# The end of the weight conversion on GpSimd, and the late units' activations turned by TensorE

## The chip, the cores and the metric

The kernel runs on one core of a Trainium2 chip. The metric is the device time of one execution in microseconds (us), median of the runs. Engines are named as the profile names them: PE is TensorE (PEld its weight loads), DVE is VectorE, ACT is ScalarE, POOL is GpSimd, SP is SyncE, which issues most of the DMAs here.

## What is computed

An mLSTM cell over 4 batches, 8 heads, 768 positions, head size 40; its output, 3072 tokens of 320 channels, goes through a multiplicative feed-forward network. From the reference, shortened:

```
for t in range(S):                       # mLSTM cell, per batch and head
    m_new  = maximum(f[t] + m, i[t])
    f_stab = exp(f[t] + m - m_new);  i_stab = exp(i[t] - m_new);  m = m_new
    C = f_stab * C + i_stab * outer(v[t], k[t])
    n = f_stab * n + i_stab * k[t]
    y[t] = sigmoid(o_gate[t]) * (C @ q[t]) / maximum(abs(n . q[t]), 1)

x = y as (3072 tokens, 320 channels)
h = ((x @ w1) * (x @ w2)) @ w3           # w1, w2: 320 x 1024, w3: 1024 x 1024
out = h @ w_out                          # 1024 x 320
```

The four weights arrive in float64; everything else is float32.

## The kernel before

**Units and steps.** The cell is computed in chunks. A unit is 128 positions of one batch (all 8 heads): 24 units, unit n being batch n mod 4. One loop of 30 steps, counted from 0, pipelines everything. Step s does the scores and the state update of unit s and the outputs of unit s-1 (both in `quarter_work`, into one PSUM tile named cell), turns the output y of an earlier unit into xT (channels on partitions), runs some of the up products (`up`, `up_rest`: x @ w1 into pa and x @ w2 into pb, multiplied into ab), and from step 17 on some of the down products (`ffn_out`: ab @ w3o into po, then the output DMA). `n_up` and `n_down` say how many of each: one up in steps 3 to 6, two from step 7 on; two downs in steps 17 to 26.

**Order.** TensorE's instructions are chained in program order (`in_order`). For the other engines a scheduler orders them by priorities, `tc.issue_after` moving some behind others; for everything up to and including step 6 (`pinned = 7`), `keep_order` fixes them in program order as well. In one step VectorE does: L348 (scores times weights), L352 and L357 (state), L368 and L372 (h), L377 to L380 (den), L382 and L384 (y), then conversions, and L568 (ab). GpSimd does: L280 (two selects on pw of the next unit), L302 (vw), L307 (decay of the state, twice a unit: once ahead of the step's products, once between L352 and L357), L412 (the doubling of y's last 64 channels).

**From y to xT.** For units 0 to 14 (n < NY = 15) `twice` copies y's last 64 channels behind themselves on GpSimd (L412), so that the last, half-filled block of channels lies on both halves of the partitions, and `x_trans` turns three blocks of 128 on TensorE into px and copies px to xT on ScalarE (L422). For units 15 to 23 `send` and `get_back` write y to DRAM and read it back in another order, and `x_turn` transposes it on VectorE (L408).

**Conversion of weights.** A weight piece of 128 x 512 (or 128 x 320 for w_out) comes as pairs of 32-bit words into raw (four buffers; `fetch`). `scale` (L175, ScalarE) scales the high words in place. `to_f32` then makes float32 out of both words in five passes on VectorE: L186 and L187 put sign and shifted exponent and mantissa into t (tile ex), L188 keeps the sign and exponent of t in r (tile ma), L189 multiplies the low words into r, L190 adds t and r into the result. `n_cvt` says how many conversions follow in each step: two in step 4 and 5, three in steps 6 to 8, two after that, to step 15. Pieces of w1 and w2 come first, then w_out, then two for each of eight blocks of w3; the latter are transposed on VectorE (L239, w3T), and `fold` makes w3o = w3 @ w_out of them on TensorE (`w3_mm`, into wp), a block a step, in steps 10 to 17.

**PSUM.** pa, pb, px, pt, wp and po share four banks in turn; cell has four of its own. After step 24 these are added to the turn.

**Names in the profile.** Tiles are named as in the code: gates is one tile of [128, 2 * TB] that holds the gate vectors at the start and, from unit 17 on, the k and q that are loaded for `turn`; between them it is not used.

Of the kernel before, what the change touches and what calls it, by code (L numbers as in the profile page):

```python
# [8 lines left out]
FP = mybir.dt.float32  # L9
U32 = mybir.dt.uint32  # L10
AF = mybir.ActivationFunctionType
OP = mybir.AluOpType
# [4 lines left out]
def kernel(  # L17
# [91 lines left out]
    wT = const.tile([P, NT2, BH], FP, name="wT")  # L109
    decay = const.tile([P, B * NP, NT], FP, name="decay")  # L110
    U_d = dram.tile([NT, BH, L], FP, name="U_d")
    NY = 15
    KC = KF + 1
    y_d = [dram.tile([P, 4, KC, 32], FP, name=f"y_d{n}") if n >= NY else None for n in range(NU)]

    o_t, u_t = {}, {}

# [56 lines left out]
        hi = raw[:, :, 1].bitcast(FP)  # L174
        nc.scalar.mul(out=hi, in_=hi, mul=2.0 ** -111)  # L175

    def to_f32(dst, raw):

        n = dst.shape[-1]
        lo, hi = raw[:, :, 0], raw[:, :, 1]
        t = wst.tile([128, n], U32, name="ex", tag="ex", bufs=1)
        r = wst.tile([128, n], U32, name="ma", tag="ma", bufs=1)
        V = nc.vector
        V.tensor_scalar(out=t, in0=hi, scalar1=3, scalar2=None, op0=OP.logical_shift_left)  # L186
        V.scalar_tensor_tensor(out=t, in0=hi, scalar=0x80000000, in1=t, op0=OP.bitwise_and, op1=OP.bitwise_or)  # L187
        V.tensor_scalar(out=r, in0=t, scalar1=0xFF800000, scalar2=None, op0=OP.bitwise_and)  # L188
        V.scalar_tensor_tensor(out=r.bitcast(FP), in0=lo, scalar=2.0 ** -52, in1=r.bitcast(FP), op0=OP.mult, op1=OP.mult)  # L189
        V.tensor_tensor(out=dst, in0=t.bitcast(FP), in1=r.bitcast(FP), op=OP.add)  # L190

    def cols(c0, n):
# [32 lines left out]
        scaled.append(pend.pop(0))  # L225
        scale(scaled[-1][1])

    def convert():
        if not scaled:
            scale_next()  # L230
        dst, raw, ko, half = scaled.pop(0)
        if dst is not None:
            to_f32(dst, raw)
            return
        w3 = wst.tile([128, CW], FP, name="w3", tag="w3")
        to_f32(w3, raw)
        if half == 0:
            w3T_t[ko] = wst.tile([128, FO, 128], FP, name="w3T", tag="w3T")
        nc.vector.transpose(out=w3T_t[ko].rearrange("c k (m r) -> c m k r", r=32)[:, 2 * half:2 * half + 2],  # L239
                            in_=w3.rearrange("r (m k c) -> r m k c", m=2, k=FO))  # L240
        if half:
            turned_w3.append(ko)

    def fold():
# [54 lines left out]
    def weighted(n):  # L299
        c, b = divmod(n, B)  # L300
        vw_t[n] = sb.tile([P, H, D1], FP, name="vw", tag="vw")
        nc.gpsimd.tensor_tensor(out=vw_t[n], in0=vbuf[n % NB], op=OP.mult,  # L302
                                in1=wT[:, c, b * H:(b + 1) * H].unsqueeze(2).to_broadcast([P, H, D1]))

    def decayed(new, old, n, x):
        c, b = divmod(n, B)
        nc.gpsimd.tensor_tensor(out=new, in0=old, op=OP.mult, in1=decay[:, b * NP:(b + 1) * NP, 2 * c + x:2 * c + x + 1]  # L307
                                .to_broadcast([P, NP, D1]))
# [55 lines left out]
    def outputs(n, pi, ph):  # L364
# [6 lines left out]
        for x, r in enumerate(halves):  # L371
# [11 lines left out]
        y_t[n] = sb.tile([P, DM + REM], FP, name="y", tag="y")  # L383
        return nc.vector.tensor_tensor(out=y_t[n][:, 0:DM].rearrange("p (h d) -> p h d", d=D), in0=h[:, :, 0:D], in1=e,  # L384
                                op=OP.mult)

    def send(n):


        y = y_t.pop(n)  # L390
        for cc in range(KF):
            nc.sync.dma_start(out=y_d[n][:, :, cc, :], in_=y[:, cc * P:(cc + 1) * P].rearrange("t (i c) -> t i c", c=32))
        for i in range(0, 4, 2):
            nc.sync.dma_start(out=y_d[n][:, i:i + 2, KF, :], in_=y[:, KF * P:DM].rearrange("t (i c) -> t i c", c=32))

    back_t = {}

    def get_back(n):
        back_t[n] = sb.tile([P, 4, KC, 32], FP, name="yb", tag="yb", bufs=1)
        for i in range(4):  # L400
            nc.sync.dma_start(out=back_t[n][32 * i:32 * (i + 1)].rearrange("r m k c -> r m (k c)"),
                              in_=y_d[n][:, i].rearrange("(m r) k c -> r m (k c)", r=32))

    def x_turn(n):
        gr, j = divmod(n, GT)
        if j == 0:
            x_t[gr] = ffn.tile([128, KC, TG], FP, name="xT", tag="xT")
        nc.vector.transpose(out=x_t[gr][:, :, j * P:(j + 1) * P].rearrange("c k (m r) -> c k m r", r=32),  # L408
                            in_=back_t.pop(n).rearrange("r m k c -> r k m c"))

    def twice(n):
        nc.gpsimd.tensor_copy(out=y_t[n][:, DM:DM + REM], in_=y_t[n][:, KF * P:DM])  # L412
# [173 lines left out]
    w12 = [("w12", i, part) for part in range(2) for i in range(2 * KF + 1)]  # L586
    todo = w12[KF * 2 + 1:] + [("wo", i, 0) for i in range(FO)] + [("w3", ko, part) for ko in range(FO) for part in range(2)]
    n_cvt = [2, 1, 1, 1, 2, 2, 3, 3, 3] + [2] * 7
    pinned = 7
    behind = ExitStack()  # L590
    turned, converted, fetched = 0, 2, 2 * KF + 1

    for s in range(len(n_up)):
        if B <= s + 3 < NU:
            load_u(s + 3)
        if s + 2 < NU:
            load(s + 2)
            load_o(s + 2)
        if 0 < s < B - 1:
            weights(s + 1)  # L600
            out_gate(s)
        if s < NU:
            weighted(s)
            if s >= B:
                decayed(state[s % B][1], state[s % B][0], s, 0)
            if 0 < s < N_DVE:
                turn(s)
        if NY <= s - 2 < NU:
            send(s - 2)
        elif 0 <= s - 2 < NY:  # L610
            twice(s - 2)
        if N_DVE <= s + 1 < NU:
            load_turned(s + 1)
        if NY <= s - 2 < NU:
            get_back(s - 2)
        while turned < min(s - 2, NY):
            x_trans(turned)
            turned += 1
        fold()
        for _ in range(n_down[s]):  # L620
            ffn_out(*downs.pop(0))
        now = [ups.pop(0) for _ in range(n_up[s])]
        open_ups = [up(*x) for x in now]
        if len(now) == 1 and turned == s - 2 < NY:
            x_trans(turned)
            turned += 1

        def rest():
            for x in open_ups:
                up_rest(*x)  # L630

        gated = None
        if s <= NU:
            gated = quarter_work(s, rest)
        else:
            rest()
        with tc.issue_after(gated.ins) if gated else nullcontext():
            if NY <= s - 2 < NU:
                x_turn(s - 2)
            if N_DVE <= s + 1 < NU:  # L640
                turn(s + 1)
        if s == 0:
            gate_cols(g, gT, nc.scalar.copy)
            out_gate(0)
            scale_next()
            weights(1)
        if s == NU:
            cell_psum.close()
            banks.append(ctx.enter_context(tc.tile_pool(name="ps_x", bufs=4, space=bass.MemoryType.PSUM)))
        if B - 1 <= s < NU:  # L650
            if s + 1 < NU:
                weights(s + 1)
            out_gate(s)
        for _ in range(n_cvt[s] if s < len(n_cvt) else 0):
            convert()
            converted += 1
        while todo and fetched < converted + (2 if s < 2 else 3):
            fetch(*todo.pop(0))
            fetched += 1
        if s + 1 == pinned:  # L660
            for ins in keep_order(front):
                behind.enter_context(tc.issue_after(ins))
# [30 lines left out]
```

## Time and profile before

| | |
|---|---|
| median of 3 runs | 485.59 us (484.08 to 487.2) |
| the profiled execution: time | 485.59 us |
| the profiled execution: span of the trace | 483.8 us |
| mean granted clock of TensorE | 0.975 |
| busy: PE, PEld, DVE, ACT, POOL | 94%, 77%, 55%, 29%, 18% of the span |
| DMA | 49.31 MB, mean 102 GB/s |

The span is what the trace covers, from the first to the last instruction; the time of the execution is 1.8 us longer. The page gives busy shares of the whole span and of 40 slices, the chain of work that ended last, and groups of instructions by line and tile. A timeline line reads: start, length, engine, line, operation, output<-inputs, shapes, how many, and in brackets how long the engine had been idle before it and what ended that. A line of the waits reads: engine, line, what it waited for, us in total, times, longest. Busy time by stretch gives, for each engine, busy us and instructions in brackets, then the granted TensorE clock, the busy share of the DMA engines, and GB/s.

### The profile page before, as it was taken

The numbers are of one execution on the slowest core, as the hardware profiler recorded it, in microseconds if no ns is written. First come the engines' busy times: TensorE is split into PE (matmuls) and PEld (weight loads), VectorE is DVE, ScalarE is ACT, GpSimd is POOL, SyncE is SP. The second block draws the span as 40 slices with busy tenths as digits, with TensorE's granted clock in tenths as the row PEclk, the third lists the DMA queues.
The fourth block names the chain that finished last, engine by engine and source line by source line (L and its number), as shares of the span: only waits on it lengthen the run. The fifth ranks groups of instructions, "written<-read, shape, count | busy, mean of one in ns | idle before, by whom it ended". The sixth has DMA issues, their size and how long they took to land.

```text
span 483.8 us, 13400 instructions
## 1 busy us (share of the span) xinstructions
PE 453.1 (94%) x5631; PEld 370.5 (77%) x5631; DVE 265.3 (55%) x535; ACT 142.0 (29%) x390; POOL 85.8 (18%) x156
## 2 busy tenths in 40 slices
PE   3859897989899999999999999999999999999997
PEld 2758786989687887888877787877877778778864
DVE  7886698899859788877660515336154242211110
ACT  3733553633433442524531212021100011011011
POOL 5431222712303211322320202110000000000000
PEclk9797998989899999999999999999999999999999
DMA  8999937678955947630455255462331211200001
GB/s 182 175 182 214 164 88 141 119 151 192 189 107 128 182 100 154 134 82 15 87 109 115 58 122 127 96 134 54 89 93 24 62 31 31 61 14 15 1 15 41
DMA packets 135772, 49.31 MB, mean 102 GB/s; under 512 B 116320, under 2 KB 126752, under 8 KB 135712
## 3 DMA queue, kind: packets, MB, share of 16 engines
q1 hardware_dynamic: 132112, 44.42, 46.8%
q10 hardware_dynamic: 3600, 4.03, 2.4%
q8 instruction: 44, 0.72, 0.7%
q14 instruction: 16, 0.13, 0.1%
HBM read 42.63 MB, written 5.80 MB: 100 GB/s over the span
## 4 chain that ended last, share of the span: by engine, by line
PE 75%; DVE 11%; issue 6%; DMA 3%; POOL 2%; SPq 1%; ACT 1%; DVEq 0%; POOLq 0%; ACTq 0%
PE po L90 22%; PE pa L90 21%; PE pb L90 14%; PE wp L90 8%; PE cell L90 7%; PE pt L93 2%; DVE h L372 2%; DMA pw<-U_d 1%; DMA kbuf<-in_k_dram 1%; PE ub L90 1%; SPq L170 1%; DVE ma L189 1%; DVE ex L187 1%; DVE o_in L382 1%; POOL pw L280 1%
## 5 line engine op out<-in xcount | busy, mean ns | idle before, releaser
L568 DVE TENSOR_TENSOR ab<-pb,a_sb 128x512 f32<-128x512 f32 x48 | 32.9, 690 | 149.6 <-ACT a_sb L567 149.4
L90 PE MATMUL po<-w3o,ab 128*128 128x320 f32 x384 | 106.2, 435 | 0.0
L90 PEld LDWEIGHTS po<-w3o,ab 128*128 128x128 f32 x384 | 72.1, 190 | 30.1 <-issue 0.4
L90 PE MATMUL pa<-xT,w 128*128 128x256 f32 (+1 forms) x448 | 94.2, 358 | 0.7 <-ACT xT L422 0.7
L90 PE MATMUL pb<-xT,w 128*128 128x256 f32 (+1 forms) x448 | 92.5, 353 | 0.7 <-issue 0.7
L90 PEld LDWEIGHTS pa<-xT,w 128*128 128x128 f32 x448 | 78.2, 199 | 11.8 <-ACT xT L422 1.1
L90 PEld LDWEIGHTS pb<-xT,w 128*128 128x128 f32 x448 | 76.8, 194 | 8.4
L567 ACT ACTIVATE a_sb<-pa 128x512 f32<-128x512 f32 x48 | 28.6, 597 | 148.2 <-PE pb L90 148.2
L90 PE MATMUL pa<-xT,wr 64*64 64x256 f32 (+1 forms) x448 | 48.2, 357 | 0.0
L90 PE MATMUL pb<-xT,wr 64*64 64x256 f32 (+1 forms) x448 | 48.2, 357 | 0.0
L307 POOL TENSOR_TENSOR state<-state,decay 128x164 f32<-128x164 f32 x40 | 19.5, 492 | 150.1 <-issue 53.7
L278 ACT ACTIVATE pw<-pw,aT 128x64 f32<-128x64 f32 x160 | 40.6, 337 | 18.2 <-DMA pw<-U_d 18.2
L280 POOL TENSOR_SCALAR_AFFINE_SELECT pw<-pw 64x512 f32<-64x512 f32 x48 | 36.5, 760 | 46.8 <-ACT pw L278 45.2
L90 PEld LDWEIGHTS pa<-xT,wr 64*64 64x64 f32 x448 | 29.2, 136 | 15.0 <-issue 7.0
L90 PE MATMUL wp<-wo,w3T 128*128 128x320 f32 x128 | 37.5, 448 | 2.0 <-DVE w3T L239 2.0
L90 PEld LDWEIGHTS wp<-wo,w3T 128*128 128x128 f32 x128 | 24.6, 197 | 11.8 <-issue 3.5
L575 ACT COPY o_sb<-po 128x320 f32<-128x320 f32 x24 | 10.2, 424 | 76.9 <-PE po L90 76.9
L90 PEld LDWEIGHTS cell<-vbuf,pw 64*64 64x64 f32 x768 | 26.9, 139 | 4.2 <-issue 2.0
L90 PEld LDWEIGHTS pb<-xT,wr 64*64 64x64 f32 x448 | 29.2, 136 | 0.0
L90 PE MATMUL cell<-vbuf,pw 64*64 64x41 f32 x768 | 26.8, 228 | 1.4 <-issue 1.4
L348 DVE TENSOR_TENSOR pw<-cell,pw 128x512 f32<-128x512 f32 x24 | 16.4, 684 | 15.7 <-PE cell L90 13.2
L372 DVE TENSOR_TENSOR h<-cell,h 64x328 f32<-64x328 f32 x48 | 23.8, 497 | 1.0
(90 smaller groups left out, 481.3 us busy)
## 6 DMA issues: line engine op xcount, KB each, us to landing
raw<-in_moe_w_dram SPq DMA_DIRECT2D x64, 128.0 KB, 3.2
pw<-U_d SPq DMA_DIRECT2D x40, 128.0 KB, 3.9
kbuf<-in_k_dram SPq DMA_DIRECT2D x24, 160.0 KB, 4.0
vbuf<-in_v_dram SPq DMA_DIRECT2D x24, 160.0 KB, 4.8
o_in<-in_o_gate_dram SPq DMA_DIRECT2D x24, 160.0 KB, 3.4
out_dram<-o_sb ACTq DMA_DIRECT2D x24, 160.0 KB, 2.0
raw<-in_moe_w_dram SPq DMA_DIRECT2D x7, 512.0 KB, 5.9
qbuf<-in_q_dram SPq DMA_DIRECT2D x17, 160.0 KB, 4.9
```

Source lines behind the costliest of these rows:

```text
L90: in_order(nc.tensor.matmul(out, lhsT=lhsT, rhs=rhs, start=start, stop=stop))
L93: in_order(nc.tensor.transpose(out, in_, ident[0:n, 0:n]))
L170: nc.sync.dma_start(out=dst, in_=src)
L187: V.scalar_tensor_tensor(out=t, in0=hi, scalar=0x80000000, in1=t, op0=OP.bitwise_and, op1=OP.bitwise_or)
L278: nc.scalar.activation(out=pw[:, h, :], in_=src[:, h, :], func=AF.Exp, bias=aT[:, c, b * H + h:b * H + h + 1])
L280: nc.gpsimd.affine_select(out=pw[r], in_=pw[r], compare_op=OP.is_ge, fill=0.0, base=0, pattern=[[0, H], [1, L]], channel_multiplier=-1)
L307: nc.gpsimd.tensor_tensor(out=new, in0=old, op=OP.mult, in1=decay[:, b * NP:(b + 1) * NP, 2 * c + x:2 * c + x + 1] .to_broadcast([P, NP, D1]))
L348: first_read = nc.vector.tensor_tensor(out=pv, in0=ss, in1=pv, op=OP.mult)
L372: nc.vector.tensor_tensor(out=h[r], in0=ph[x], in1=h[r], op=OP.add)
L567: nc.scalar.mul(out=a_sb, in_=pa, mul=UP ** -2)
L568: nc.vector.tensor_tensor(out=ab_t[gr][j][:, fs[0]:fs[-1] + 1, t0:t0 + a_sb.shape[-1]], in0=pb, in1=a_sb, op=OP.mult)
L575: nc.scalar.copy(out=o_sb, in_=po)
```

## The change

Two things are changed.

In steps 4 to 14 the last two conversions of each step take another form (`to_f32` with E). t and r are no longer tiles of their own but the first two slices of 512 columns of gates, the same two for every such conversion. The three first passes stay on VectorE. ScalarE then scales the low words in place, and the last two passes, a product and a sum, run on GpSimd. A piece of w3 converted so is transposed a step later (`unturned`, `turn_w3`), and with it `fold` comes to that block a step later. GpSimd's share of unit n for n > 4 (`weigh`: L302 and the first L307) is written at the end of step n-1, ahead of the conversions, instead of at the start of step n.

Units 15 to 23 no longer go through DRAM: `send`, `get_back` and `x_turn` are gone, and `twice` and `x_trans` serve all 24 units.

```
@@ -109,9 +109,7 @@
     wT = const.tile([P, NT2, BH], FP, name="wT")
     decay = const.tile([P, B * NP, NT], FP, name="decay")
     U_d = dram.tile([NT, BH, L], FP, name="U_d")
-    NY = 15
     KC = KF + 1
-    y_d = [dram.tile([P, 4, KC, 32], FP, name=f"y_d{n}") if n >= NY else None for n in range(NU)]
 
     o_t, u_t = {}, {}
 
@@ -174,19 +172,27 @@
         hi = raw[:, :, 1].bitcast(FP)
         nc.scalar.mul(out=hi, in_=hi, mul=2.0 ** -111)
 
-    def to_f32(dst, raw):
+    def to_f32(dst, raw, E=None):
 
 
 
         n = dst.shape[-1]
         lo, hi = raw[:, :, 0], raw[:, :, 1]
-        t = wst.tile([128, n], U32, name="ex", tag="ex", bufs=1)
-        r = wst.tile([128, n], U32, name="ma", tag="ma", bufs=1)
+        if E is None:
+            t = wst.tile([128, n], U32, name="ex", tag="ex", bufs=1)
+            r = wst.tile([128, n], U32, name="ma", tag="ma", bufs=1)
+        else:
+            t, r = (gates[:, i * CW:i * CW + n].bitcast(U32) for i in range(2))
         V = nc.vector
         V.tensor_scalar(out=t, in0=hi, scalar1=3, scalar2=None, op0=OP.logical_shift_left)
         V.scalar_tensor_tensor(out=t, in0=hi, scalar=0x80000000, in1=t, op0=OP.bitwise_and, op1=OP.bitwise_or)
         V.tensor_scalar(out=r, in0=t, scalar1=0xFF800000, scalar2=None, op0=OP.bitwise_and)
-        V.scalar_tensor_tensor(out=r.bitcast(FP), in0=lo, scalar=2.0 ** -52, in1=r.bitcast(FP), op0=OP.mult, op1=OP.mult)
+        if E is None:
+            V.scalar_tensor_tensor(out=r.bitcast(FP), in0=lo, scalar=2.0 ** -52, in1=r.bitcast(FP), op0=OP.mult, op1=OP.mult)
+        else:
+            V = E
+            nc.scalar.mul(out=lo.bitcast(FP), in_=lo, mul=2.0 ** -52)
+            V.tensor_tensor(out=r.bitcast(FP), in0=lo.bitcast(FP), in1=r.bitcast(FP), op=OP.mult)
         V.tensor_tensor(out=dst, in0=t.bitcast(FP), in1=r.bitcast(FP), op=OP.add)
 
     def cols(c0, n):
@@ -225,20 +231,30 @@
         scaled.append(pend.pop(0))
         scale(scaled[-1][1])
 
-    def convert():
+    def convert(E=None):
+
         if not scaled:
             scale_next()
         dst, raw, ko, half = scaled.pop(0)
         if dst is not None:
-            to_f32(dst, raw)
+            to_f32(dst, raw, E)
             return
         w3 = wst.tile([128, CW], FP, name="w3", tag="w3")
-        to_f32(w3, raw)
-        if half == 0:
+        to_f32(w3, raw, E)
+        if ko not in w3T_t:
             w3T_t[ko] = wst.tile([128, FO, 128], FP, name="w3T", tag="w3T")
+        if E is None:
+            turn_w3(w3, ko, half)
+        else:
+            unturned.append((w3, ko, half))
+
+    unturned, halves_in = [], {}
+
+    def turn_w3(w3, ko, half):
         nc.vector.transpose(out=w3T_t[ko].rearrange("c k (m r) -> c m k r", r=32)[:, 2 * half:2 * half + 2],
                             in_=w3.rearrange("r (m k c) -> r m k c", m=2, k=FO))
-        if half:
+        halves_in[ko] = halves_in.get(ko, 0) + 1
+        if halves_in[ko] == 2:
             turned_w3.append(ko)
 
     def fold():
@@ -384,30 +400,6 @@
         return nc.vector.tensor_tensor(out=y_t[n][:, 0:DM].rearrange("p (h d) -> p h d", d=D), in0=h[:, :, 0:D], in1=e,
                                 op=OP.mult)
 
-    def send(n):
-
-
-        y = y_t.pop(n)
-        for cc in range(KF):
-            nc.sync.dma_start(out=y_d[n][:, :, cc, :], in_=y[:, cc * P:(cc + 1) * P].rearrange("t (i c) -> t i c", c=32))
-        for i in range(0, 4, 2):
-            nc.sync.dma_start(out=y_d[n][:, i:i + 2, KF, :], in_=y[:, KF * P:DM].rearrange("t (i c) -> t i c", c=32))
-
-    back_t = {}
-
-    def get_back(n):
-        back_t[n] = sb.tile([P, 4, KC, 32], FP, name="yb", tag="yb", bufs=1)
-        for i in range(4):
-            nc.sync.dma_start(out=back_t[n][32 * i:32 * (i + 1)].rearrange("r m k c -> r m (k c)"),
-                              in_=y_d[n][:, i].rearrange("(m r) k c -> r m (k c)", r=32))
-
-    def x_turn(n):
-        gr, j = divmod(n, GT)
-        if j == 0:
-            x_t[gr] = ffn.tile([128, KC, TG], FP, name="xT", tag="xT")
-        nc.vector.transpose(out=x_t[gr][:, :, j * P:(j + 1) * P].rearrange("c k (m r) -> c k m r", r=32),
-                            in_=back_t.pop(n).rearrange("r m k c -> r k m c"))
-
     def twice(n):
         nc.gpsimd.tensor_copy(out=y_t[n][:, DM:DM + REM], in_=y_t[n][:, KF * P:DM])
 
@@ -586,9 +578,14 @@
     w12 = [("w12", i, part) for part in range(2) for i in range(2 * KF + 1)]
     todo = w12[KF * 2 + 1:] + [("wo", i, 0) for i in range(FO)] + [("w3", ko, part) for ko in range(FO) for part in range(2)]
     n_cvt = [2, 1, 1, 1, 2, 2, 3, 3, 3] + [2] * 7
-    pinned = 7
+    pinned, early = 7, 4
     behind = ExitStack()
     turned, converted, fetched = 0, 2, 2 * KF + 1
+
+    def weigh(n):
+        weighted(n)
+        if n >= B:
+            decayed(state[n % B][1], state[n % B][0], n, 0)
 
     for s in range(len(n_up)):
         if B <= s + 3 < NU:
@@ -600,20 +597,15 @@
             weights(s + 1)
             out_gate(s)
         if s < NU:
-            weighted(s)
-            if s >= B:
-                decayed(state[s % B][1], state[s % B][0], s, 0)
+            if s <= early:
+                weigh(s)
             if 0 < s < N_DVE:
                 turn(s)
-        if NY <= s - 2 < NU:
-            send(s - 2)
-        elif 0 <= s - 2 < NY:
+        if 0 <= s - 2 < NU:
             twice(s - 2)
         if N_DVE <= s + 1 < NU:
             load_turned(s + 1)
-        if NY <= s - 2 < NU:
-            get_back(s - 2)
-        while turned < min(s - 2, NY):
+        while turned < min(s - 2, NU):
             x_trans(turned)
             turned += 1
         fold()
@@ -621,7 +613,7 @@
             ffn_out(*downs.pop(0))
         now = [ups.pop(0) for _ in range(n_up[s])]
         open_ups = [up(*x) for x in now]
-        if len(now) == 1 and turned == s - 2 < NY:
+        if len(now) == 1 and turned == s - 2 < NU:
             x_trans(turned)
             turned += 1
 
@@ -635,8 +627,6 @@
         else:
             rest()
         with tc.issue_after(gated.ins) if gated else nullcontext():
-            if NY <= s - 2 < NU:
-                x_turn(s - 2)
             if N_DVE <= s + 1 < NU:
                 turn(s + 1)
         if s == 0:
@@ -651,8 +641,12 @@
             if s + 1 < NU:
                 weights(s + 1)
             out_gate(s)
-        for _ in range(n_cvt[s] if s < len(n_cvt) else 0):
-            convert()
+        if early <= s < NU - 1:
+            weigh(s + 1)
+        while unturned:
+            turn_w3(*unturned.pop(0))
+        for i in range(n_cvt[s] if s < len(n_cvt) else 0):
+            convert(nc.gpsimd if i + 2 >= n_cvt[s] and early <= s < len(n_cvt) - 1 else None)
             converted += 1
         while todo and fetched < converted + (2 if s < 2 else 3):
             fetch(*todo.pop(0))
```

## The prediction

> **What bounds the kernel now.** Steps are counted from 0; step s does the quarter work of unit s. I read the engine totals first, then busy time by step (cut at the starts of L348, the first thing VectorE does with a step's scores), then the waits of TensorE, then the timelines of the steps where it waits.
>
> ```profile
> PE 453.1 (94%) x5631; PEld 370.5 (77%) x5631; DVE 265.3 (55%) x535; ACT 142.0 (29%) x390; POOL 85.8 (18%) x156
> ```
>
> 94% is a mean over stages. By step, from L348 of step 3 to L348 of step 11, and later, over nine full steps:
>
> ```profile
> 48.71:60.19 11.48, 9.11 (x205) 8.32 (x205) 8.10 (x18) 6.48 (x18) 3.19 (x6) 1.00 1.07 162
> 60.19:72.32 12.13, 11.12 (x227) 10.60 (x226) 10.94 (x22) 6.34 (x17) 3.25 (x6) 1.00 0.39 90
> 72.32:83.64 11.32, 8.02 (x184) 7.27 (x184) 10.12 (x23) 3.55 (x12) 3.25 (x6) 0.85 0.76 140
> 83.64:101.26 17.62, 15.39 (x281) 14.97 (x280) 16.06 (x35) 10.29 (x31) 8.93 (x14) 0.93 0.62 122
> 101.26:112.87 11.61, 11.61 (x255) 11.42 (x255) 10.75 (x27) 4.11 (x13) 3.65 (x6) 0.96 0.98 188
> 112.87:126.97 14.10, 13.57 (x214) 11.63 (x211) 13.10 (x28) 6.83 (x18) 2.64 (x5) 1.00 0.92 195
> 126.97:147.03 20.06, 18.25 (x215) 14.41 (x216) 13.11 (x28) 5.71 (x16) 2.86 (x5) 0.91 0.69 125
> 147.03:163.80 16.77, 16.77 (x221) 13.81 (x220) 14.17 (x30) 6.62 (x19) 3.99 (x7) 1.00 0.76 150
> ...
> 271.40:411.00 139.60, 139.60 (x1446) 109.75 (x1445) 53.59 (x108) 21.92 (x56) 10.14 (x17) 1.00 0.36 80
> ```
>
> Columns: length, busy PE, PEld, DVE, ACT, POOL, clock, DMA. VectorE sets the pace from step 4 to about 128 us; from step 10 on TensorE has no gap, so there only its own instructions count. Where TensorE waits:
>
> ```profile
> PE px L93 <- DVE y L384: 4.5, 3, 3.3
> ...
> PE pt L93 <- DVE ab L568: 2.2, 1, 2.2
> PE wp L90 <- DVE w3T L239: 2.0, 1, 2.0
> ```
>
> Step 5 of the timeline, GpSimd and then TensorE, carries the forecast:
>
> ```profile
> 61.20 0.47 POOL L307 TENSOR_TENSOR state<-state,decay 128x164 f32<-128x164 f32 x1 [6.69 <-DVE state L352]
> 61.61 1.38 POOL L280 TENSOR_SCALAR_AFFINE_SELECT pw<-pw 64x512 f32<-64x512 f32 x2
> 63.07 0.74 POOL L302 TENSOR_TENSOR vw<-vbuf,wT 128x328 f32<-128x328 f32 x1
> 63.77 0.46 POOL L307 TENSOR_TENSOR state<-state,decay 128x164 f32<-128x164 f32 x1
> 65.61 0.36 POOL L412 COPY y<-y 128x64 f32<-128x64 f32 x1 [1.38 <-DVE y L384]
> ...
> 65.69 0.67 PE L93 MATMUL px<-ident,y 128*128 128x128 f32 x3 [1.01 <-DVE y L384]
> ```
>
> y of unit 3 ends on VectorE at 65.55 (65.06 + 0.49), GpSimd doubles its tail at once (L412), and the third px transpose reads that tail. TensorE is in order: behind px stand the rest of the up products, then cell, then L348. So step 5 hangs on a loop: L348, y, L412, px, cell, next L348.
>
> What idling costs TensorE, one step later:
>
> ```profile
> 75.00:77.80 2.80, 0.00 (x0) 1.00 1.38 186
> 77.80:79.50 1.70, 1.68 (x23) 0.63 0.48 116
> 79.50:81.50 2.00, 2.00 (x44) 0.50 0.20 49
> 81.50:83.60 2.10, 2.10 (x112) 0.97 0.52 159
> ```
>
> [...] L302 at 328 elements takes 0.74, L307 at 164 takes 0.46, so 512 by the line through them is 1.05. [...] on 96x256 tiles L506 takes 0.42, L508 and L510 0.72 and 0.83 while GpSimd runs L507 and L509. [...] Above, 3.3 us of idling is followed by 0.50. [...] Seen above: L307 waits 6.69 us to 61.20, and the selects behind it start only then, though their ScalarE input was complete at 58.48 (56.47 + 2.01).
>
> **The change part by part.** In steps 4 to 14 two conversions each (22 in all) lose L189 and L190 on VectorE and get one ScalarE scaling and two GpSimd passes. That frees VectorE 0.69 + 0.69 a conversion of 512 columns, about 30 us in all. But the two new tiles are fixed slices of gates, one set for all. The order of instructions on each engine shows what follows:
>
> (a) VectorE's first pass of the second conversion (B) overwrites what GpSimd's last pass of the first (A) reads, so it waits. In series now: A's three passes on VectorE, two on GpSimd, B's three, two on GpSimd.
>
> (b) On GpSimd the four passes of step s stand ahead of the L412 copy that belongs to step s+1. In steps 5 and 6, where px needs that copy in the same step, px waits for all of (a). In step 7 the px of that unit comes only in step 8; nothing waits.
>
> Step 4 to 5, from L348 at 60.19. y ends 65.55, A's passes (0.42, 0.69, 0.43, starting 65.46) end 67.07. GpSimd: start after 0.08, as L307 after L352 here; two passes at 1.1[...] to 69.35. B to 71.04, GpSimd to 73.32, copy to 73.66. From third px to L348: 3.72 here at full clock (65.98 to 69.7), but TensorE has then idled 7 us, so I take the 5.35 of the next step (78.10 to 83.45), which followed such an idle. L348 at 79.0 instead of 72.32: +6.7. Step 5 to 6, counted from its L348: A (512) done 6.88, GpSimd 9.16, B (320 columns: 0.33, 0.49, 0.33) 10.45, GpSimd 2 x 0.74 to 12.05, copy 12.38, plus 5.35 gives 17.7 against 11.32: +6.4. Together +13.1.
>
> Steps 6 to 10. VectorE's sum from L348 of step 6: chain to y 5.4; the conversion still whole 2.25; A 1.2; wait 1.7; B 1.2; three passes 1.2; ab 0.7. That makes 13.6, where ab releases the qT transposes (L93) at 98.62 - 83.64 = 15.0 today: TensorE 1.4 ahead, less idle. In step 7 GpSimd is late (selects, vw and decays stand behind the conversions), which costs VectorE about 2.6 us of waiting at B; in step 9 the transposes wait for ab until 42.5 on this count. Then comes a gain: the first w3T is now turned a step later, so step 10 has no wp, and neither the 2.0 us wait nor its slow start (6.24 where the later ones take 4.31) arises. The up products of step 10 start at 43.3 on this count, against 51.0 today, of which 4.3 is the wp that moves to step 17. -3.4 at best, -1.8 if the clock dips; I take -3.0.
>
> Steps 11 to 17 stay at 16.8: VectorE with its two waits of 2.3 comes to about 15, and w3T is ready a step ahead. ScalarE's 22 scalings at the 0.635 of L175 (14 us) lie in an engine busy 40% of these steps.
>
> Units 15 to 23: nine times three transposes return to TensorE, where nothing hides them. At 163.92 px starts and wp at 164.24: 0.33 each, +3.0. Taken away are nine VectorE transposes of 0.57 and 72 DMA issues on SP, and added are nine copies on GpSimd and nine on ScalarE: all beside a TensorE that never waits here, worth nothing either way.
>
> Moving vw and the first decay a step earlier costs nothing by itself: GpSimd did them at that place already (63.07). Its raw tiles come free later by some 2 us; they are fetched a step ahead, so 0, or +2 if ScalarE's queue stands behind a late one.
>
> Sum: 13.1 - 3.0 + 3.0 = +13.1. The profiled execution took 485.59 with a span of 483.8, and 485.59 is also the median: 498.7.
>
> Bounds. A GpSimd pass could be 1.05 (-0.4 on eight passes) or 1.3 (+1.5[...]). A warm clock would take 3.2 off. Steps 6 to 10 lie between -8 and +3.
>
> **The rivals.** (1) The forecast, 498.7. (2) The relief decides: VectorE stops being the bound from step 6 to 10 and TensorE runs back to back: steps of 12.4, 12.7 and 12.4 plus 1.2 to step 10's first up product are 38.7 where today's count is 46.7: -8.0. Speaking for it are the VectorE shares of those steps; against it, the serial waits of (a). With the queue at +13.1 it gives 493.7; with a clock that also stays warm, 490.5, about 1% slower. (3) Faster or level: GpSimd is so quick that the queue costs nothing. The two steps then are 25.2 + 7.3p (p is one pass of 512; the sum above with p left open) against 23.45, warm. With rival 2's -8.0 and the +3.0 it turns at p = 0.45; at 0.3 it gives 484.5. Two-input passes in this trace are far above that. (4) The change as meant, copy not behind the conversions: steps 5 and 6 would gain 1.0, total 484.6. The order on GpSimd speaks against it. (5) The late copies and waits spread: VectorE past 16.8 in steps 11 to 16 by 1 us each: 504.7.
>
> **How the numbers follow.** Forecast 0.62, rival 2 0.17, rivals 3 and 4 0.03 each, rival 5 0.15. About 1% is what a measurement of this kernel can tell from no change. Slower by over 1%: rivals 1 and 5 and most of 2, 0.89; within 1%: 0.08; faster: 0.03. The range runs from rival 2 with a clock partly warm (491) to near rival 5 (504).
>
> **What would show it.** Right: in steps 5 and 6 px waits for GpSimd's y copy, some 7 us each, half clock after it, those steps 17 to 19 us long; VectorE waits for GpSimd at the first pass of every second conversion; no wp in step 10, two in step 17; from step 11 on TensorE full, about 0.33 longer a step from step 18. Wrong: if these two steps stay under 14 us, or if steps 6 to 9 shrink by more than 5, or if TensorE has gaps after step 11.

## The result, and the profile after

The changed kernel takes 512.1 us, the median of 4 runs (509.07 to 513.54), against 485.78 for the kernel before: a ratio of 1.0535, 95% interval 1.047 to 1.06. The forecast was 498.7 with a range up to 504, so the sign was right and the size was half of what happened. The profiled execution of the changed kernel took 509.07 with a span of 507.4. It is the quickest of the four; the sums below are made against spans, 507.4 - 483.8 = 23.6.

Line numbers moved with the edit: y is now L400 (was L384), the first work on a step's scores L364 (L348), the y copy L404 (L412), ab L560 (L568), the decay of the state L323 (L307). The engine totals of after first:

```profile
PE 460.1 (91%) x5658; PEld 375.7 (74%) x5658; DVE 237.2 (47%) x482; ACT 158.4 (31%) x421; POOL 135.4 (27%) x209
```

VectorE has 28.1 us less work (265.3 before), and TensorE's busy share fell from 94% to 91%. Busy time by stretch of after, cut at the starts of L364 of steps 4, 5 and 6, at that of step 17, and at the end (columns as before: length, PE, PEld, DVE, ACT, POOL, clock, DMA share, GB/s):

```profile
60.19:79.88 19.69, 10.31 (x204) 9.62 (x204) 8.24 (x18) 5.27 (x16) 8.16 (x10) 0.74 0.64 115
79.88:99.75 19.87, 11.64 (x204) 10.90 (x204) 7.85 (x18) 7.52 (x21) 7.35 (x10) 0.71 0.45 81
99.75:290.81 191.06, 184.44 (x2511) 153.57 (x2512) 118.04 (x240) 81.96 (x217) 86.32 (x113) 0.99 0.54 111
290.81:507.40 216.59, 212.01 (x1851) 164.12 (x1850) 58.05 (x115) 34.42 (x81) 11.84 (x25) 1.00 0.18 45
```

The same two long stretches of before:

```profile
83.64:271.50 187.86, 183.29 (x2511) 153.68 (x2510) 136.99 (x277) 73.10 (x202) 47.52 (x76) 0.98 0.59 121
271.50:483.80 212.30, 209.02 (x1824) 161.52 (x1824) 62.24 (x124) 30.11 (x72) 10.04 (x17) 1.00 0.26 61
```

These cuts are worth copying: TensorE has the same 2511 instructions between step 6 and step 17 in both kernels (the block of wp products that moved to step 17 stays inside), so the lengths can be subtracted. In both kernels step 4 starts its scores' work at 60.19. So the 23.6 us are: steps 4 and 5, 39.56 against 23.45 (12.13 + 11.32), +16.1; steps 6 to 16, 191.06 against 187.86, +3.2; the rest, 216.59 against 212.30, +4.3. The forecast had +13.1, -3.0 and +3.0.

What TensorE and VectorE wait for in after:

```profile
DVE w3T L254 <- POOL w L196: 18.4, 7, 2.9
...
PE px L93 <- POOL y L404: 15.6, 2, 8.4
...
PE pt L93 <- DVE ab L560: 4.2, 5, 1.9
...
DVE gates L187 <- POOL w L196: 2.8, 1, 2.8
...
PE po L90 <- DVE h L388: 1.3, 1, 1.3
```

The second line is the queue that the forecast named: px of steps 5 and 6 waits 15.6 us in two pieces for a copy of 0.24 us. GpSimd in step 5, then the px that it releases:

```profile
67.20 1.29 POOL L195 TENSOR_TENSOR gates<-raw,gates 128x512 f32<-128x512 f32 x1 [2.97 <-issue]
68.56 1.26 POOL L196 TENSOR_TENSOR w<-gates 128x512 f32<-128x512 f32 x1
71.61 1.29 POOL L195 TENSOR_TENSOR gates<-raw,gates 128x512 f32<-128x512 f32 x1 [1.78 <-issue]
72.97 1.26 POOL L196 TENSOR_TENSOR w<-gates 128x512 f32<-128x512 f32 x1
74.18 0.24 POOL L404 COPY y<-y 128x64 f32<-128x64 f32 x1
...
74.47 0.47 PE L93 MATMUL px<-ident,y 128*128 128x128 f32 x1 [8.38 <-POOL y L404]
```

y itself is ready on VectorE at 65.54 (65.05 + 0.49). Between the second and the third line VectorE does the three first passes of the next conversion, and starts them only when GpSimd has left the shared tile:

```profile
69.86 0.43 DVE L187 TENSOR_SCALAR gates<-raw 128x512 uint32<-128x512 uint32 x1 [2.79 <-POOL w L196]
```

The first and the last line of the waits above were not in the forecast. The experiments are about them.

### The profile page after: what moved, and what is told of

It is laid out like the page before. It is cut to its first block, busy times and chain, and to the rows that moved or that the text cites. A ratio compares the mean times of both kernels' runs of the same rounds, so it can differ in the third digit from the quotient of the medians.

```text
span 507.4 us, 13428 instructions
## 1 busy us (share of the span) xinstructions
PE 460.1 (91%) x5658; PEld 375.7 (74%) x5658; DVE 237.2 (47%) x482; ACT 158.4 (31%) x421; POOL 135.4 (27%) x209
## 4 chain that ended last, share of the span: by engine, by line
PE 68%; POOL 5%; issue 5%; DVE 4%; DMA 2%; ACT 1%; SPq 1%; POOLq 0%; DVEq 0%; ACTq 0%
PE po L90 20%; PE pa L90 19%; PE pb L90 13%; PE cell L90 7%; PE wp L90 6%; POOL gates L195 2%; PE pt L93 2%; PE px L93 1%; DMA raw<-in_moe_w_out_dram 1%; DMA qbuf<-in_q_dram 1%; ACT pw L294 1%; POOL w L196 1%; SPq L168 1%; POOL pw L296 1%; DVE h L388 1%
## 5 line engine op out<-in xcount | busy, mean ns | idle before, releaser
L560 DVE TENSOR_TENSOR ab<-pb,a_sb 128x512 f32<-128x512 f32 x48 | 32.8, 689 | 168.9 <-ACT a_sb L559 168.6
L559 ACT ACTIVATE a_sb<-pa 128x512 f32<-128x512 f32 x48 | 28.6, 597 | 143.3 <-PE pb L90 143.3
L323 POOL TENSOR_TENSOR state<-state,decay 128x164 f32<-128x164 f32 x40 | 19.2, 485 | 112.7 <-PE cell L90 65.5
L195 POOL TENSOR_TENSOR gates<-raw,gates 128x512 f32<-128x512 f32 (+1 forms) x22 | 26.6, 1209 | 52.8 <-DVE gates L189 17.6
L296 POOL TENSOR_SCALAR_AFFINE_SELECT pw<-pw 64x512 f32<-64x512 f32 x48 | 33.3, 694 | 25.4 <-ACT pw L294 23.7
L90 PE MATMUL wp<-wo,w3T 128*128 128x320 f32 x128 | 35.8, 434 | 0.7 <-DVE ab L560 0.7
L93 PE MATMUL px<-ident,y 128*128 128x128 f32 x72 | 13.9, 295 | 18.3 <-POOL y L404 15.6
L404 POOL COPY y<-y 128x64 f32<-128x64 f32 x24 | 6.6, 275 | 86.8 <-DVE y L400 86.5
```

The lines of the kernel that those rows point to most:

```text
L90: in_order(nc.tensor.matmul(out, lhsT=lhsT, rhs=rhs, start=start, stop=stop))
L93: in_order(nc.tensor.transpose(out, in_, ident[0:n, 0:n]))
L195: V.tensor_tensor(out=r.bitcast(FP), in0=lo.bitcast(FP), in1=r.bitcast(FP), op=OP.mult)
L296: nc.gpsimd.affine_select(out=pw[r], in_=pw[r], compare_op=OP.is_ge, fill=0.0, base=0, pattern=[[0, H], [1, L]], channel_multiplier=-1)
L559: nc.scalar.mul(out=a_sb, in_=pa, mul=UP ** -2)
L560: nc.vector.tensor_tensor(out=ab_t[gr][j][:, fs[0]:fs[-1] + 1, t0:t0 + a_sb.shape[-1]], in0=pb, in1=a_sb, op=OP.mult)
```

## Experiments

Theory Q was the forecast's: the y copy stands behind GpSimd's passes. Its rival S laid the two long steps to the tiles that the conversions share. What the forecast had not seen, in steps 6 to 13, got theory T later: VectorE's transposes of w3 wait for GpSimd, with ab behind them in the queue. Rival R laid that to the raw weights arriving late. The stage columns are the spans of the three stretches above, from each kernel's own trace; TensorE's instruction count for the middle one is 2511 in all. The start of the first stretch lies between 59.7 and 62.4 us. Each ratio is to runs of the kernel before on the same chip. Behind each stage length stands one trace. Where two kernels have the same code up to the end of a stage, their lengths still differ by up to 1.8 us (steps 4 and 5: 23.01 in both, 24.77 in late_turn; steps 6 to 16: 187.86 in before, 188.94 in y_only), so one or two us between two traces show little by themselves.

| kernel | time, us | ratio to before, 95% | steps 4, 5 | steps 6 to 16 | rest |
|---|---|---|---|---|---|
| before | 485.8 | | 23.45 | 187.86 | 212.30 |
| after | 512.1 | 1.0535 [1.047, 1.06] | 39.56 | 191.06 | 216.59 |
| copy_first | 496.96 | 1.0219 [1.0172, 1.0265] | 24.94 | 194.33 | 217.96 |
| two_sets | 507.36 | 1.043 [1.0391, 1.0469] | 38.03 | 191.78 | 216.35 |
| both | 494.61 | 1.018 [1.0143, 1.0218] | 23.01 | 193.41 | 216.36 |
| y_only | 492.11 | 1.011 [1.007, 1.015] | 24.80 | 188.94 | 216.28 |
| late_turn | 490.5 | 1.0091 [1.0067, 1.0116] | 24.77 | 188.37 | 216.37 |
| conv_only | 504.81 | 1.0387 [1.0337, 1.0437] | 39.74 | 191.30 | 212.31 |
| conv_late | 487.02 | 1.0016 [0.9991, 1.0042] | 23.13 | 187.53 | 212.25 |
| conv_early | 486.64 | 1.0 [0.9979, 1.0021] | 23.35 | 188.30 | 212.29 |
| after_late | 505.53 | 1.0415 [1.0368, 1.0461] | 39.74 | 185.98 | 216.30 |
| copy_late | 497.69 | 1.0243 [1.0205, 1.028] | 24.61 | 193.63 | 216.28 |

**copy_first**: the y copy of steps 5 and 6 goes ahead of the conversions of the step before, all else as in after.

```
-        if 0 <= s - 2 < NU:
+        if 0 <= s - 2 < NU and s not in (5, 6):
             twice(s - 2)
...
+        if s in (4, 5):
+            twice(s - 1)
         while unturned:
```

> The changed kernel with one edit: in steps 4 and 5 the doubling of y that belongs to the next step is issued on GpSimd ahead of that step's conversions. Theory Q (px hangs on the copy that stands behind the conversion passes in GpSimd's queue): the step from the scores of unit 4 to those of unit 5 falls from 19.7 us to about 12.2, the next from 19.9 to about 11.5, no half clock there, some 16 us off in all: about 496. Rival S (the one set of tiles, which makes the conversions run in series, is what stretches those steps, wherever the copy stands): both steps stay above 17, at most 3 us off: about 509.

496.96, 15 us less than after. Its steps 4 and 5:

```profile
60.77:72.72 11.95, 11.95 (x223) 11.71 (x223) 8.16 (x18) 7.11 (x20) 6.33 (x9) 0.86 0.41 86
72.72:85.71 12.99, 8.86 (x187) 8.27 (x186) 7.84 (x19) 5.38 (x18) 8.61 (x11) 0.74 0.67 127
```

The first step is back to the length of before. The second is 1.7 over it, and close to the 12.68 of y_only, whose code up to here is that of before. The conversion passes are still on GpSimd. The half clock is less, but not gone as expected: the mean clock is 0.86 and 0.74. Q is shown: moving one 0.24 us copy is worth 39.56 - 24.94 = 14.6 us in these steps. The middle stage, however, is 3.3 longer than in after, and it is as long in both and copy_late (193.41, 193.63): part of the gain seems to be lost again there. How much is uncertain, because this trace is of the slowest of four runs and that of after of the quickest.

**two_sets**: the second conversion of a step gets its own pair of tiles, ex and ma, so that it need not wait for GpSimd; the copy stays behind.

```
-        if E is None:
+        if E is None or second:
             t = wst.tile([128, n], U32, name="ex", tag="ex", bufs=1)
             r = wst.tile([128, n], U32, name="ma", tag="ma", bufs=1)
```

> The changed kernel with a second pair of tiles (ex and ma) for the second of each step's two conversions; the copy stays behind. Theory Q: GpSimd's four passes then follow each other, so the copy comes 1.6 us earlier in step 5 and 1.3 in step 6, both steps stay above 17; VectorE's waits of 2.0 to 2.9 us for GpSimd's last pass go in steps 6 to 13, worth 3 to 6 us there: 503 to 506. Rival S: both steps fall to 12 to 13 us, 15 off: about 497.

507.36, just above what Q gave: the two steps are 20.08 and 17.95 (S had 12 to 13), 1.5 us less than in after together, and px's wait falls only from 15.6 to 13.4. The forecast's chain (a) is a small part of it; the place of the copy is the rest. S is refuted. But Q had also priced VectorE's waits in steps 6 to 13 at 3 to 6 us, to be gained here, and that failed: the transpose of w3 (L254) still waits 20.4 us for GpSimd in all, and the middle stage is 191.78 where after has 191.06.

**both**: the two edits together.

> The changed kernel with both edits: copy ahead of the conversions in steps 4 and 5, and a second pair of tiles. Theory Q with a separate cost of the waits: about 16 and 4 to 6 us off: 490 to 492, with what is left from TensorE's transposes of the late units (4.3) less a gain in steps 4 to 10. If the waits for the one set cost nothing by themselves: 496, as with the copy alone.

494.61, above what was expected. Steps 4 and 5 are right, 10.98 and 12.03, but the middle stage stays at 193.41, 5.55 over before. The timeline shows where: VectorE between 150 and 162 us, and the transposes of TensorE that need a PSUM bank which ab must free:

```profile
153.98 1.03 DVE L188 SCALAR_TENSOR_TENSOR ex<-raw,ex 128x512 uint32<-128x512 uint32 x1
155.04 0.84 DVE L189 TENSOR_SCALAR ma<-ex 128x512 uint32<-128x512 uint32 x1
158.69 0.71 DVE L254 STREAM_TRANSPOSE w3T<-w 128x512 f32<-128x512 f32 x1 [2.80 <-POOL w L196]
159.32 0.38 DVE L187 TENSOR_SCALAR gates<-raw 128x512 uint32<-128x512 uint32 x1
159.74 0.69 DVE L188 SCALAR_TENSOR_TENSOR gates<-raw,gates 128x512 uint32<-128x512 uint32 x1
160.46 0.69 DVE L560 TENSOR_TENSOR ab<-pb,a_sb 128x512 f32<-128x512 f32 x1
...
161.21 1.12 PE L93 MATMUL pt<-ident,qbuf 128*128 128x128 f32 x4 [3.81 <-DVE ab L560]
...
162.76 5.90 PE L90 MATMUL wp<-wo,w3T 128*128 128x320 f32 x16
```

ScalarE's half of the product (a_sb, L559) was complete at 154.01, and ab (L560) starts at 160.46. Ahead of it in VectorE's queue stands a transpose of w3 that waits 2.80 us for GpSimd's last pass. TensorE then stands 3.81 us and comes back at half clock (0.50 from 161.21 to 165.00): pt takes 1.12 and wp 5.90, where those before them, at 140.20 and 140.96, took 0.60 and 4.47.

**y_only**: the kernel before with y of all units turned by TensorE (`NY = 24`), no change to the conversion.

> The kernel before with NY = 24: all units are turned by TensorE, the conversion stays wholly on VectorE. Theory: nine times three transposes at 0.33 (3.0), and 1.3 for a wait of the first down product of step 25 on VectorE's h, whose place in the turn of banks moves: +4.3, about 490. Rival: the late part costs only the 3.0, about 488.6, and the 1.3 belongs to the conversion.

492.11, 1.1% over before, or 5.3 us, where 4.3 was expected; by the trace the last stage is 216.28, 4.0 over. It has 1851 TensorE instructions there instead of 1824, 27 transposes, and this line, which the kernel before hasn't:

```profile
PE po L90 <- DVE h L372: 1.3, 1, 1.3
```

In after the sum can be closed exactly: busy time 212.01 - 209.02 = 2.99, the 9 x 0.33 of the forecast, and idle time 4.58 - 3.28 = 1.30, this wait. So the 1.3 does not belong to the conversion, as the rival had it. It falls in step 25, the first after cell's four banks join the turn. With a px in each step the turn takes seven banks a step instead of six, and a po falls on a bank that the outputs h of the last unit still read. That the shift of the turn is the reason is argued from the order of allocation, not tried.

**late_turn**: `both`, and the transposes of w3 placed in VectorE's queue behind gates and y of the step.

```
-        while unturned:
-            turn_w3(*unturned.pop(0))
+        with tc.issue_after(gated.ins) if gated else nullcontext():
+            while unturned:
+                turn_w3(*unturned.pop(0))
```

> The kernel `both` (y copy ahead of the conversions in steps 4 and 5, a second pair of tiles for the second conversion), with one more edit: VectorE's transposes of w3 (L254) are placed in its queue after gates and y of the step, not ahead of ab and of the scores. Theory T: in steps 6 to 13 ab stood behind a transposition of w3, which waited 2.0 to 2.9 us for the last GpSimd pass of its piece, and in `both` this cost TensorE 6.4 us between the ups of step 11 and those of step 12 (23.2 where 16.8 is the work). Then ab starts with its own input, the wait of pt for ab near 140 to 165 us goes, and the time is 494.6 - 6.4 = 488, taken as 487 to 490. Rival R: what comes late there is the raw weights themselves, since GpSimd keeps the four raw buffers longer and the loads of the next pieces start later; then nothing changes: 493 to 496.

490.5, just above what T gave and well under R's range. The middle stage fell from 193.41 to 188.37, and TensorE's wait of pt for ab from 6.6 to 0.7. T holds for this kernel. R, by which nothing would change, falls. The longest wait of TensorE between 98 and 200 us is now another: cell waits 2.71 us for vw (L318), which stands in GpSimd's queue behind a conversion pass:

```profile
156.71 1.09 PE L90 MATMUL cell<-vw,kbuf 64*64 64x41 f32 x32 [2.71 <-POOL vw L318]
```

**after_late**: the same one edit on the changed kernel itself, to see whether T explains the miss there and not only in a kernel with two other edits.

> The changed kernel with one edit alone: VectorE's transposes of w3 stand behind gates and y of the step. The y copy stays behind the four passes, so steps 4 and 5 stay as they are (19.7 and 19.9). The loss of the change in steps 6 to 16 was 3.2 us by the two traces (191.06 where the kernel before has 187.86). Theory T, that this loss is ab behind a transpose of w3 that waits for GpSimd: steps 6 to 16 come to 187.5 to 188.5, and the time falls by 2.6 to 3.6, to 508.5 to 509.5. If the loss has another cause, such as the longer passes of VectorE beside GpSimd or the state's chain behind GpSimd's passes: no change, 511 to 513, with steps 6 to 16 at 190.5 or more.

505.53, a fall of 6.6 (1.2% by the ratios), larger than expected. The stages show it in one place, 5.1 us: steps 6 to 16 from 191.06 to 185.98, the other two as they were. The place in after, VectorE and then TensorE, and the same ab in after_late:

```profile
143.48 0.71 DVE L254 STREAM_TRANSPOSE w3T<-w 128x512 f32<-128x512 f32 x1 [2.82 <-POOL w L196]
144.22 1.29 DVE L560 TENSOR_TENSOR ab<-pb,a_sb 128x512 f32<-128x512 f32 x2
...
144.97 0.66 PE L93 MATMUL pt<-ident,qbuf 128*128 128x128 f32 x4 [1.90 <-DVE ab L560]
...
141.06 1.45 DVE L560 TENSOR_TENSOR ab<-pb,a_sb 128x512 f32<-128x512 f32 x2
```

In after the a_sb of the first ab was complete at 139.95, and ab starts 4.3 us later; TensorE waits 1.90 us, and its clock is 0.50 from 147.00 to 149.00. In after_late a_sb was complete at 140.92, ab starts at 141.06, and TensorE does not wait there. Of the 5.1 us, 3.1 are idle time of TensorE (6.62 in after, 3.55 in after_late) and 2.0 are busy time (184.44, 182.43). The slow stretch is not certain to come with the wait: in conv_only the same wait, 1.89 us, left the clock at 1.00, and the first two pa and pb that follow took no longer than the later ones (all 1.89 us), where in after they took 3.06 and 2.45. Waits of after_late:

```profile
DVE gates L187 <- POOL w L196: 19.5, 12, 2.8
...
PE pt L93 <- DVE ab L560: 1.6, 3, 0.8
```

VectorE waits for GpSimd almost as long as before (19.5 us for w in place of 18.4 + 2.8), only at another instruction, the first pass of a conversion. ab still stands behind such a wait in places, and at 190.07 starts 2.7 us after its a_sb, but from step 10 on TensorE waits at most 0.3 us at a time for it, and pt's wait falls from 4.2 to 1.6 in all. So a total of waiting time on VectorE says little; what is queued behind the wait decides. And 185.98 is 1.9 under the kernel before. The first up product of step 10 starts 43.9 us after the scores of step 6 (144.64 - 100.72), where after has 46.0 and the forecast had 43.3 at best: the relief that the forecast counted in steps 6 to 10 (-3.0) is there, once this wait does not cover it.

**copy_late**: copy_first with the same edit, the pair of tiles still shared.

> The y copy ahead in steps 4 and 5, and the transposes of w3 behind gates and y; one pair of tiles for both conversions, unlike `late_turn`. If the order alone brought the gain of `late_turn` over `both`: steps 6 to 16 at 188.4 or a little more (copy_first had 194.36), and 490 to 492.5. If the first pass of the second conversion, which waits for GpSimd's last pass where the pair of tiles is shared, still holds VectorE up there: steps 6 to 16 at 191 or more, and 493.5 or more.

497.69, no better than copy_first, middle stage 193.63. VectorE's queue shows why:

```profile
157.41 0.43 DVE L187 TENSOR_SCALAR gates<-raw 128x512 uint32<-128x512 uint32 x1 [3.31 <-DMA raw<-in_moe_w_dram]
...
162.58 0.43 DVE L187 TENSOR_SCALAR gates<-raw 128x512 uint32<-128x512 uint32 x1 [2.81 <-POOL w L196]
163.04 0.69 DVE L188 SCALAR_TENSOR_TENSOR gates<-raw,gates 128x512 uint32<-128x512 uint32 x1
163.76 0.69 DVE L560 TENSOR_TENSOR ab<-pb,a_sb 128x512 f32<-128x512 f32 x1
```

The first pass of a conversion now waits where the transpose did, because it overwrites the tile that GpSimd reads, and ab stands behind it again. The first of these lines names a load, but GpSimd's L196 ended at 157.38 (156.12 + 1.26) and this pass starts at 157.41. This is not all: cell waits 3.32 us for GpSimd's vw in this step, 0.6 more than in late_turn. So a second set of tiles, worth some 1.5 us in steps 4 and 5 (within what two traces differ by), is worth 193.63 - 188.37 = 5.3 here. Why the shared pair costs this with the copy ahead, and not in after_late, whose steps 6 to 16 come 15 us later, was not separated.

**conv_only**: after's conversion part with the DRAM route of before for units 15 to 23 (`NY = 15`, with `send`, `get_back` and `x_turn`).

> The change's conversion part alone: y of the 16th unit and later goes through DRAM as in the kernel before. With the late part of the change worth 4.3 us by the trace of after (0.33 us on each of nine steps and one wait of 1.3 us for h in step 25), 512.1 - 4.3 = 507.8, taken as 506 to 509.5. If the two parts lean on each other (VectorE of steps 17 and later late because of both), the fall is larger: under 505.

504.81, under the expected 506 and just in the range of the rival, by which the two parts lean on each other. By the stages nothing leans on anything: steps 4 and 5 and the middle are those of after within 0.3, and the rest is that of before, 212.31. The traces thus give 4.3. The ratios differ by 1.5%, or 7 us, but each is known to little better than half a per cent, from four runs of each kernel, and the traces are of the quickest run of after and the slowest of conv_only. late_turn and the next kernel, conv_late, also differ by the late part alone, with twenty runs each: 490.5 - 487.02 = 3.5 us.

**conv_late** and **conv_early** take the late part out as well. conv_late is conv_only with the three edits of late_turn; in conv_early GpSimd gets conversions only in steps 4 to 7 (`early <= s < 8`), with the copy ahead and two sets. In those steps the last two passes of both conversions run on GpSimd; the second one stays on VectorE only in its first three passes and in its tiles.

> The conversion part alone (y of the 16th unit and later through DRAM), with the three edits of `late_turn`. Theory T, with the late part worth 4.3: 488 - 4.3 = 483.7, so level with the kernel before or up to 2 us under it (482 to 486). Rival R: 494.6 - 4.3 = 490.3 (489 to 492).

> The conversion part alone, GpSimd taking the last two passes only in steps 4 to 7; from step 8 on they stay on VectorE as in the kernel before. The y copy stands ahead in steps 4 and 5, and the second conversion of a step stays on VectorE with its own pair of tiles. Theory T or R, both: the loss of steps 8 to 13 is gone, and steps 4 and 5 are what they were in `both` (10.98 and 12.03 where the kernel before has 12.13 and 11.32): 486 less 0.4, so 483 to 487. If the half clock of TensorE in steps 5 to 7 needs relief on VectorE that the waits for GpSimd take back, 488 to 490.

487.02 and 486.64: level with the kernel before, neither under it by anything the runs can tell. conv_early is as expected; conv_late is 1 us above what T gave, and 2 under R's range. In conv_late steps 4 to 16 take 210.66 us against 211.31. Little was left to gain: between step 6 and step 17 TensorE is busy 182.35 of 187.53 us in conv_late and 183.29 of 187.86 in before, so 4.6 us of idle time, and what slow clock follows it (mean clock 0.98 in before, 0.99 in conv_late), were all that relief of VectorE could have removed there. conv_late, with 5.2, removed none of the idle time: 2.7 of it is again cell waiting for GpSimd's vw, a wait that the kernel before does not have between 98 and 200 us. No version was faster than the kernel before.

## Why the prediction was right or wrong

**Right: the mechanism and the order of events in steps 4 and 5.** px of steps 5 and 6 waits for the copy (15.6 us), VectorE waits at the first pass of the second conversion (2.79), half clock follows (0.50 from 74.47 to 77.50 and from 93.03 to 99.75), two blocks of wp come in step 17, and copy_first takes the long wait away. That VectorE would wait so at every second conversion held in steps 4 to 7 only; from there on it is L254, the transpose of w3, that waits for GpSimd. Rivals 3 and 4 of the forecast needed a quick GpSimd or a copy that is not behind; neither was so. copy_first is nearly what rival 4 describes, and it took 496.96, not 484.6, so the copy's place was not all that stood between the change and a gain. Rival 2 (relief decides, -8.0) is far off: the middle stage rose. Rival 5 (late waits spread over steps 11 to 16) has the nearest number, but 5.0 of TensorE's 6.6 us of waits for ab in the middle stage come before step 10's up products; the later ones are of 0.7, 0.6 and 0.3. Gaps of TensorE after step 11 were among the forecast's own signs of being wrong.

**Readings that were off, without weight in the sum.** The last of the forecast's step windows ends at 163.80, where L348 of step 11 starts at 165.69, and the stretch from 271.40 to 411.00 holds seven steps, not nine. The 4.31 of a late wp is from its start to the next instruction; in the way that the 6.24 is counted it is 4.47. And in the kernel before, L348 of step 5 did not hang on px: the scores were complete at 69.71, and L348 started at 72.32, when VectorE had done ab ahead of it. The loop through px became the limit only with the change.

**Term 1, steps 4 to 6: +13.1 forecast, +16.1 measured.** Two prices were low. A GpSimd pass was put at 1.1 (0.74 for 320 columns); the two passes took 1.29 and 1.26 (0.88 and 0.86). On four passes a step this is 0.70 and 0.61, and the copies end 0.76 and 0.72 later than forecast. The 1.1 was the author's estimate; the trace of before gives 1.05, by the line through two shorter passes. Against the mean of the two measured passes, 1.275, they were 14% and 18% low. The bounds had held 1.3. The second is the clock: from px to L364 the forecast took 5.35 in both steps. The first took 5.41, the second 6.72. After px in both steps, in stretches:

```profile
74.47:77.50 3.03, 3.03 (x51) 2.81 (x52) 0.00 (x0) 1.07 (x3) 0.00 (x0) 0.50 1.43 171
77.50:79.88 2.38, 2.38 (x117) 2.31 (x116) 0.69 (x1) 2.38 (x11) 0.00 (x0) 0.88 0.43 94
...
93.03:95.50 2.47, 2.47 (x41) 2.25 (x41) 0.00 (x0) 0.51 (x2) 0.00 (x0) 0.50 1.38 171
95.50:98.00 2.50, 2.50 (x78) 2.50 (x78) 0.69 (x1) 2.50 (x10) 0.00 (x0) 0.50 1.26 196
98.00:99.75 1.75, 1.75 (x61) 1.63 (x56) 0.00 (x0) 1.75 (x5) 0.00 (x0) 0.50 0.19 46
```

After waits of 8.38 and 7.24 us the clock was at half for some 3.6 us in the first case (3.03, and 0.57 to make the mean 0.88 of the 2.38 after it). In the second it was at half for all of the 6.7 us and beyond, to about 102.0 (0.50 from 99.75 to 101.75, 0.94 in the two us after), some 9 us, with TensorE busy throughout. The longer wait was followed by the shorter slow stretch, so the forecast's one price for both, read off a single stretch of before, could hold for the first only.

**Term 2, steps 6 to 16: -3.0 forecast, +3.2 measured** (2.1 to 3.4 with the traces of y_only and conv_only, whose code here is that of before and of after). This is the step that failed: 6.2 of the 10.5 us that the span missed by. The forecast counted the gain of the first w3T coming a step later, and for the steps after it wrote that VectorE "with its two waits of 2.3 comes to about 15, and w3T is ready a step ahead". Its sum of VectorE's time is not what failed: after_late has the same passes and comes to within 0.6 us of the count by step 10 (43.9 for 43.3). What it left out is the place of the wait: L254 waits up to 2.9 us, and ab, which TensorE needs in the same step, stands behind it. By the first up product of step 10 this had taken 2.1 us (46.0 where after_late has 43.9), and most of the rest came after, from slow clock (0.50 from 147.00 to 149.00) and further such waits (0.7, 0.6 and 0.3). Having w3T a step ahead for TensorE does not make its transposition free for VectorE. after_late recovers 5.1 of the 6.2 by moving only this.

**Term 3, late transposes: +3.0 forecast, +4.3 measured.** The price, 9 x 0.33, held (2.99). The 1.3, which the forecast did not have, is the wait of one po for h.

So the span was short by 3.0 + 6.2 + 1.3 = 10.5. The rest of the distance to 512.1 is that the profiled run lies 3 us under the median of its kernel.

**Costs put at nothing.** Busy time and one wait make up the whole change of the last stage, so nothing of it is left for SP's 72 issues. ScalarE's scalings were not tried alone; from step 6 on none of TensorE's waits in the trace of after is put down to ScalarE. VectorE's waits for the state's decay, which stands behind the passes, grew from 11.4 us in before to 24.2 in after. They were not separated, but conv_late has 23.7 of them and is level with the kernel before.

## What to carry to other kernels

Before handing work to an engine with a queue, list what small things that queue already carries for the critical path: here a copy of 0.24 us, put behind four passes, cost 14.6 us, more than everything else together. For each wait that a change adds, ask not how long it is but what stands behind it on the same engine; nearly the same 20 us of waiting on VectorE cost 5 us more in after than in after_late, where ab was no longer behind the long ones. And when one of two such waits is taken away alone, look whether the other takes its place (copy_late) before calling it harmless.

## What the runs showed of the hardware

Two of VectorE's small instructions got about as long as the GpSimd pass that ran beside them (1.30 and 1.44 us, beside 1.30 and 1.51). VectorE in after, in one step with such a pass and in a later one without, and GpSimd at the time of the first:

```profile
165.15 1.30 DVE L395 TENSOR_SCALAR den<-den 128x8 f32<-128x8 f32 x1
167.50 1.44 DVE L400 TENSOR_TENSOR y<-h,o_in 128x320 f32<-128x320 f32 x1
...
185.54 0.17 DVE L395 TENSOR_SCALAR den<-den 128x8 f32<-128x8 f32 x1
186.51 0.49 DVE L400 TENSOR_TENSOR y<-h,o_in 128x320 f32<-128x320 f32 x1
...
165.12 1.30 POOL L195 TENSOR_TENSOR gates<-raw,gates 128x512 f32<-128x512 f32 x1 [2.22 <-DVE den L393]
...
167.07 1.51 POOL L196 TENSOR_TENSOR w<-gates 128x512 f32<-128x512 f32 x1
```

An instruction on eight columns took 1.30 us instead of 0.17: it starts 0.03 after L195 and ends 0.03 after it. What ties it to the pass beside it, the traces do not show. On the chain to y this cost 2 us in that step (1.13 + 0.95).

The second thing is the clock above: 3.6 us of half speed after one wait, some 9 after another that was even a little shorter, for a reason that these traces do not show. It was no accident of one run: after_late, with the same two waits (8.37 and 7.24), has some 9 us of half clock after the second as well, from 93.99 to about 103.1. In conv_only, whose waits are also 8.37 and 7.24, TensorE's two sets of pt still take 1.11 and 1.06 us at 101.34 and 102.24, where those at 114.97 and 116.40 take 0.66 each.
